# Decayed attention and two gated layers on one core: turns for VectorE and GpSimd in the planner, small products on ScalarE, token sums on VectorE

## The chip, the core and the metric

One core of a Trainium2 chip runs the whole program. The time is device microseconds of one execution. PE is TensorE, PEld its weight load, DVE VectorE, ACT ScalarE, POOL GpSimd and SP SyncE, which issues the DMAs. The tolerance on the result is that of a float32 computation, so every matmul operand is split into a high half that TensorE keeps exactly and a low half for the rest, and each product is made of three matmuls.

## What is computed

Inputs are q, k, v (2 batches, 8 heads, 768 tokens, 64 features), a decay per head, and the weights of two layers (512 to 2048 and back), all in float32 or, for the weights, wider.

```python
# decayed attention, by blocks; lam is one number per head
intra = (q_b @ k_b.T * decay_mask) @ v_b
inter = (q_b * lam_pow) @ kv_state
out_b = intra + inter
kv_state = lam_block * kv_state + (k_b * rev_pow).T @ v_b
# first layer, on 1536 tokens x 512
h = x @ w_in;  g = h * clip(h + 3, 0, 6) / 6;  x = g @ w_out
# second layer
h = maximum(x @ w_in, 0);  y = h * h @ w_out
```

## The kernel before

**Attention** goes through 12 chunks of 128 tokens, two batches in turn. For a chunk TensorE makes the scores (L353), the product of scaled queries with the old state (L385), the product of decayed keys and values for the new state (L403), and scores times values (L437). VectorE masks the scores (L364), adds the new state to the decayed old one (L423), and takes the low half of the chunk's output (L453) after ScalarE has taken a plain copy and the high half (L448, L450). The output bank is one of two, and it is free again only after the low half: so L385 of chunk c + 2 waits for L453 of chunk c. GpSimd scales the queries (`qs`, L327), decays the keys (`kd`, L338, from the second to last chunks of each batch nothing is kept) and decays the old state (`kvs`, L416).

**The layers** take 1536 tokens as three blocks of 512 and w_in and w_out as 64 tiles of 128 x 512 (32 a layer and half a matrix each). A tile comes as 8-byte numbers and is decoded: two reads of the raw words on ScalarE (`da` L513, `dt` L517), a clamp, a shift and a join on VectorE (L522, L528, L532), the high half on ScalarE (L535), an addition and the low half on VectorE (L536, L539). A hidden unit (L666) is 12 matmuls of 512 columns; its gate follows on ScalarE (`gs`, L641) and VectorE (L644), then the halves of the result (L649 ScalarE, L651 VectorE). Four such tiles later the output products (L752) run and are added up in SBUF (L776). From the second group of four on, blocks 0 and 1 are multiplied two by two with sums of weights and of tokens (L697, seven quarter products instead of eight): the weight sums are `Tsum` (L560), `Th`, `Tl` (L573), and the token sums are `s` (L593) with their halves `Ssum` and, for the last, `xh`, `xl` (L609 on GpSimd for the first layer, L611 on VectorE for the second, L613 ScalarE).

**What sets the order.** The kernel is not written in the order of its instructions. `Plan.op` records each with an engine, a cost of `COST` (time the engine is held, time until the result is there), the operations it needs and the buffers it takes and gives. TensorE's order is fixed by hand; `dues` gives every other operation the latest time by which TensorE's order wants it. `run` then walks through time: of all engines the one that can start earliest gets its ready operation with the earliest start, and among those the earliest due. The list that comes out is the order in each engine's queue. At run time each engine works its queue in order and waits on semaphores only for data and buffers. SP's queue holds the loads, a chunk as four DMAs.

Of the kernel before, what the change touches and what calls it, by code (L numbers as in the profile page):

```python
# [9 lines left out]
F32 = mybir.dt.float32  # L10
# [4 lines left out]
AF = mybir.ActivationFunctionType  # L15
ALU = mybir.AluOpType
PSUM = bass.MemoryType.PSUM

P = 128
# [5 lines left out]
    "psc": 1.10, "inter": 1.02, "pst": 0.61, "av": 0.88, "unit": 2.72, "high": 1.81, "low": 0.91, "part": 1.36,  # L25
# [19 lines left out]
class Op:  # L45
    def __init__(self, engine, cost, do, needs, take, give, due, then):
        self.engine, self.do, self.needs, self.take, self.give = engine, do, list(needs), take, give
        cost = COST[cost] if isinstance(cost, str) else cost
        self.busy, self.lasts = cost if isinstance(cost, tuple) else (cost, cost + DRAIN)
        self.due, self.then, self.start, self.end, self.number = due, then, None, None, 0  # L50


class Plan:
# [37 lines left out]
    def run(self):  # L91
# [13 lines left out]
        order, left = [], len(self.ops)  # L105
        while left:
            best = None
            for e in clock:
                if e == "PE":
                    some = [pe[0]] if pe and not waiting[pe[0].number] else []  # L110
                else:
                    some = ready[e]
                first, pick = None, None
                for o in some:
                    t = max(clock[e], o.ready)
                    ok = True
                    for h in o.take:
                        if h.slot is None:
                            if not h.room.free:
                                ok = False  # L120
                                break
                            t = max(t, h.room.free[0][1])
                    if not ok:
                        continue
                    key = (round(t, 3), o.due, o.number)
                    if first is None or key < first:
                        first, pick = key, o
                if pick is not None and (best is None or first[0] < best[0]):
                    best = (first[0], e, pick)
            if best is None:  # L130
                stuck = [(o.engine, o.what) for o in ([pe[0]] if pe else [])]
                raise RuntimeError(f"the plan is stuck: {left} left, {stuck}")
            t, e, o = best
            o.start, o.end = t, t + o.lasts
            clock[e] = t + o.busy
            for h in o.take:
                h.slot = h.room.free.popleft()[0] if h.slot is None else h.slot
# [27 lines left out]
def decay_attention_moe_moe(  # L165
# [134 lines left out]
    def attention():  # L300
# [22 lines left out]
        def prepare(c):  # L323
            if c > 1:

                def do():
                    nc.gpsimd.tensor_tensor(  # L327
                        qs_t[:, qs_hold[c].slot].rearrange("p a i -> p (a i)"), part(c, "q"),
                        lpow_t[0].rearrange("p a i -> p (a i)"), op=ALU.mult,
                    )  # L330

                qs_hold[c] = Hold(qs_room)
                chunk_hold[c].left += 1
                qs_op[c] = op("POOL", "p512", do, [loaded[c, "q"], *scans], take=[qs_hold[c]], give=[chunk_hold[c]])
            if c < NC - 2:

                def do():
                    nc.gpsimd.tensor_tensor(  # L338
                        kd_t[:, kd_hold[c].slot], part(c, "k").rearrange("p (h d) -> p h d", d=D),
                        decay.rearrange("p a t i -> p (a t) i")[:, :, P - 1 : P].to_broadcast([P, H, D]), op=ALU.mult,  # L340
                    )

                kd_hold[c] = Hold(kd_room)
                kd_op[c] = op("POOL", "p512b", do, [loaded[c, "k"], *decays], take=[kd_hold[c]])

# [46 lines left out]
        def new_state(c):  # L392
# [18 lines left out]
            else:  # L411
                s = Hold(ts_room)

                def scale():
                    kvs_t[c] = tile_of([P, KD, HALF], F32, "Ts", f"kvs{c}")[:, :, :D]
                    nc.gpsimd.tensor_tensor(  # L416
                        kvs_t[c], kv_old, lpow_t[0][:, :, P - 1 : P].to_broadcast([P, NP, D]), op=ALU.mult
                    )
# [79 lines left out]
    def decode(n, key, uses, summed, gate):  # L498
# [21 lines left out]
        clamp = op(  # L520
            "DVE", "v512s",
            lambda: nc.vector.tensor_scalar(  # L522
# [4 lines left out]
        shift = op(  # L527
            "DVE", "v512s", lambda: nc.vector.tensor_scalar(u(), u(), 3, None, op0=ALU.logical_shift_left), [clamp]  # L528
        )
        join = op(  # L530
            "DVE", "v512",
            lambda: nc.vector.scalar_tensor_tensor(u(), r(1), -(2**31), u(), op0=ALU.bitwise_and, op1=ALU.bitwise_or),  # L532
            [shift], give=[raw],
        )
        hi = op("ACT", "s512", lambda: nc.scalar.copy(tile_w(0), u().bitcast(F32)), [join], give=[a])  # L535
        add = op("DVE", "v512", lambda: nc.vector.tensor_tensor(up(), u(), up(), op=ALU.add), [join, low], give=[a])  # L536
        lo = op(
            "DVE", "v512",
            lambda: nc.vector.tensor_tensor(tile_w(1), up().bitcast(F32), tile_w(0).bitcast(F32), op=ALU.subtract),  # L539
# [40 lines left out]
    def token_sums(layer, old):  # L580
# [54 lines left out]
    def gate(layer, j, f, ps, done, bank):  # L635
# [10 lines left out]
        else:  # L646
# [3 lines left out]
        lo = op(  # L650
            "DVE", "v512", lambda: nc.vector.tensor_tensor(gt(1), s(), gt(0).bitcast(F32), op=ALU.subtract), [hi], give=[st]  # L651
        )
# [86 lines left out]
    def project(layer, j, g, e):  # L739
# [42 lines left out]
        if layer == 0:  # L782
# [4 lines left out]
            lo = op(  # L787
                "DVE", "v512",
                lambda: nc.vector.scalar_tensor_tensor(  # L789
# [143 lines left out]
```

## Time and profile before

| what | value |
|---|---|
| median of 3 runs | 581.58 us (580.63 to 581.73) |
| profiled execution | 582.72 us, its span 580.9 us |
| TensorE busy | 557.8 us, 96% |
| VectorE busy | 416.0 us, 72% |
| ScalarE busy | 322.5 us, 56% |
| GpSimd busy | 138.3 us, 24% |
| chain that ended last | TensorE 57%, VectorE 28%, ScalarE 7%, GpSimd 2% |

The span runs from the first instruction to the last; the profiled execution's own time has 1.8 us more around it. A busy share is an average over stages with different limits, and a TensorE that is busy is not one at its peak: its matmuls overlap, so a product of 12 matmuls is best read from start to start. The rows that matter are those that say which instruction ended an idle time, stage by stage.

### The profile page before, as it was taken

What the parts mean: (1) busy time and instruction counts of PE and PEld (TensorE: products, weight loads), DVE (VectorE), ACT (ScalarE), POOL (GpSimd) and SP (SyncE); (2) the same over time, 40 slices, a digit from 0 to 9 for tenths busy, and PEclk for the clock granted to TensorE, in tenths of its full rate; (3) what the DMA queues carried; (4) which work ended last, traced back from release to release, by engine and by line L of the source; (5) the groups of instructions that cost most, each with busy time, mean ns of one, the idle gap of its engine ahead of it and who ended that gap; (6) DMA issues with size and microseconds to landing.
All of it is one profiled execution on the core that took longest, in us unless ns stands there. A gap on an engine that the chain in (4) does not pass through costs nothing.

```text
span 580.9 us, 7789 instructions
## 1 busy us (share of the span) xinstructions
PE 557.8 (96%) x2950; PEld 457.3 (79%) x2950; DVE 416.0 (72%) x635; ACT 322.5 (56%) x545; POOL 138.3 (24%) x108
## 2 busy tenths in 40 slices
PE   8969699999999999999999998999999999999997
PEld 5857487888878888788887887888877888888885
DVE  7897999817995599838999886317894589546322
ACT  2524486638751585337763796548862695358220
POOL 4878504301132104201015004201212112210000
PEclk9999799999999999999999999999999999999999
DMA  8990233301231024202231042102231042100112
GB/s 319 408 361 3 73 109 104 113 1 65 81 108 37 0 74 144 73 0 73 73 109 36 21 160 73 37 2 72 73 108 37 0 146 73 37 0 1 63 65 90
DMA packets 18037, 49.79 MB, mean 86 GB/s; under 512 B 2128, under 2 KB 2128, under 8 KB 18000
## 3 DMA queue, kind: packets, MB, share of 16 engines
q1 hardware_dynamic: 17856, 49.04, 24.1%
q8 instruction: 23, 0.38, 0.3%
q10 hardware_dynamic: 144, 0.26, 0.1%
q14 instruction: 14, 0.11, 0.1%
HBM read 46.14 MB, written 3.15 MB: 85 GB/s over the span
## 4 chain that ended last, share of the span: by engine, by line
PE 57%; DVE 28%; ACT 7%; issue 4%; POOL 2%; DVEq 0%; POOLq 0%; ACTq 0%
PE b L752 31%; PE b L697 16%; PE b L666 7%; DVE da L532 4%; DVE dt L536 4%; DVE gs L644 3%; DVE da L528 3%; DVE acc L776 2%; DVE da L522 2%; POOL Tsum L560 1%; DVE wo L539 1%; PE b L353 1%; ACT gs L648 1%; DVE xl L789 1%; DVE A L364 1%
## 5 line engine op out<-in xcount | busy, mean ns | idle before, releaser
L776 DVE TENSOR_TENSOR acc<-acc,b 128x512 f32<-128x512 f32 x72 | 48.6, 681 | 51.9 <-PE b L752 51.9
L666 PE MATMUL b<-xh,wi 128*128 128x512 f32 x240 | 78.6, 398 | 5.4 <-DVE gs L644 5.4
L752 PE MATMUL b<-gC,wo 128*128 128x512 f32 x228 | 70.2, 390 | 1.2 <-DVE gs L644 1.2
L752 PE MATMUL b<-wo,gC 128*128 128x512 f32 x228 | 68.9, 390 | 1.5 <-ACT gC L649 1.5
L666 PEld LDWEIGHTS b<-xh,wi 128*128 128x128 f32 x240 | 46.2, 193 | 15.7 <-DVE gs L644 5.8
L560 POOL TENSOR_TENSOR Tsum<-dt,dt 128x256 f32<-128x256 f32 x12 | 12.7, 1061 | 185.6 <-DVE dt L536 131.2
L573 POOL TENSOR_TENSOR Tl<-Tsum,Th 128x1024 fp32r<-128x1024 f32 x12 | 29.6, 2465 | 111.8 <-ACT Th L568 111.8
L532 DVE SCALAR_TENSOR_TENSOR da<-raw,da 128x512 int32<-128x512 int32 x64 | 50.9, 806 | 1.2
L752 PEld LDWEIGHTS b<-wo,gC 128*128 128x128 f32 x228 | 42.6, 188 | 10.9 <-ACT gC L649 1.9
L752 PEld LDWEIGHTS b<-gC,wo 128*128 128x128 f32 x228 | 42.7, 188 | 10.6 <-DVE gs L644 1.7
L536 DVE CUSTOM_DVE_ANT_0 dt<-da,dt 128x1024 uint16<-128x1024 uint16 x64 | 49.7, 784 | 1.7 <-ACT gs L648 0.2
L647 ACT ACTIVATE gs<-b 128x512 f32<-128x512 f32 x48 | 28.2, 591 | 37.6 <-PE b L666 15.0
L513 ACT ACTIVATE da<-raw 128x512 f32<-128x512 f32 x64 | 42.0, 669 | 11.6 <-issue 6.3
L641 ACT ACTIVATE gs<-b,three 128x512 f32<-128x512 f32 x48 | 32.6, 686 | 27.6 <-PE b L697 16.3
L666 PE MATMUL b<-xl,wi 128*128 128x512 f32 x120 | 47.7, 397 | 0.0
L644 DVE SCALAR_TENSOR_TENSOR gs<-gs,b 128x512 f32<-128x512 f32 x48 | 32.5, 681 | 17.5 <-ACT gs L641 17.3
L517 ACT ACTIVATE dt<-raw 128x512 int32<-128x512 uint32 x64 | 42.6, 667 | 2.1 <-DVE wikd L539 1.1
L651 DVE TENSOR_TENSOR gC<-gs,gC 128x512 fp32r<-128x512 f32 x38 | 29.4, 779 | 18.4 <-ACT gC L649 18.4
L528 DVE TENSOR_SCALAR da<-da 128x512 int32<-128x512 int32 x64 | 40.0, 625 | 1.7
L752 PE MATMUL b<-g,wo 128*128 128x512 f32 x120 | 39.0, 390 | 0.0
L752 PE MATMUL b<-wo,g 128*128 128x512 f32 x120 | 37.6, 389 | 0.0
L752 PE MATMUL b<-gA,wo 128*128 128x512 f32 x108 | 36.3, 390 | 1.1 <-DVE gs L644 1.1
(131 smaller groups left out, 1240.9 us busy)
## 6 DMA issues: line engine op xcount, KB each, us to landing
raw<-in_w_in SPq DMA_DIRECT2D x32, 512.0 KB, 3.3
raw<-in_w_out SPq DMA_DIRECT2D x32, 512.0 KB, 3.3
out<-acc SPq DMA_DIRECT2D x12, 256.0 KB, 2.0
inC<-in_kT SPq DMA_DIRECT2D x6, 256.0 KB, 5.2
inC<-in_k SPq DMA_DIRECT2D x6, 256.0 KB, 5.3
inC<-in_v SPq DMA_DIRECT2D x6, 256.0 KB, 5.4
inS<-in_kT SPq DMA_DIRECT2D x6, 256.0 KB, 5.8
inS<-in_qT SPq DMA_DIRECT2D x6, 256.0 KB, 5.9
```

Of the source, the lines that this page charges most:

```text
L513: "ACT", "s512r", lambda: nc.scalar.activation(abs_t[a.slot], r(1).bitcast(F32), AF.Abs, scale=2.0**16),
L517: "ACT", "s512r", lambda: nc.scalar.activation(up(), r(0).bitcast(U32), AF.Copy, scale=2.0**-29),
L528: "DVE", "v512s", lambda: nc.vector.tensor_scalar(u(), u(), 3, None, op0=ALU.logical_shift_left), [clamp]
L532: lambda: nc.vector.scalar_tensor_tensor(u(), r(1), -(2**31), u(), op0=ALU.bitwise_and, op1=ALU.bitwise_or),
L536: add = op("DVE", "v512", lambda: nc.vector.tensor_tensor(up(), u(), up(), op=ALU.add), [join, low], give=[a])
L573: "POOL", "p1024", lambda: nc.gpsimd.tensor_tensor(at["l"], at["f"], at["h"].bitcast(F32), op=ALU.subtract),
L641: a = op("ACT", "s512b", lambda: nc.scalar.activation(s(), ps(), AF.Relu, bias=three), [done], take=[st])
L644: lambda: nc.vector.scalar_tensor_tensor(s(), s(), 6.0, ps(), op0=ALU.min, op1=ALU.mult), [a], give=bank,
L666: nc.tensor.matmul(ps(), u, x[:, a, :], start=a == 0 and i == 0, stop=a == KD - 1 and i == 2)
L697: nc.tensor.matmul(t, p0, p1, start=start and a == 0 and n == 0, stop=a == KH - 1 and n == 2, skip_group_check=True,)
L752: nc.tensor.matmul(ps(), u, y, start=f == fs[0] and i == 0, stop=f == fs[-1] and i == 2)
L776: "DVE", "v512", lambda: nc.vector.tensor_tensor(t(), t(), ps(), op=ALU.add), [low, old[e]], give=[bank],
```

## The change

Four things change. (1) The planner gets a clock named `port`: an operation on GpSimd, or one on VectorE whose cost name begins with `d`, can start only when the last of these has left it. GpSimd's candidates are dropped where a ready VectorE operation of that kind has an earlier due time and could start before GpSimd's would end. The `d` names go to VectorE's instructions that read and write SBUF alone: the decode steps, the low halves of gates and of the layer's output. (2) The decayed keys become eight ScalarE instructions of 64 columns a chunk, each with a scale read per partition, and the decayed states four. (3) The token sums `s` go from GpSimd to VectorE (four in each layer), and the first layer's low halves too. (4) Costs are renamed or added. Nothing else in the text differs; SP's order is the same.

```diff
+    "d512": (0.60, 0.69), "d512s": (0.36, 0.44), "d256": (0.335, 0.42), "d1024": (1.13, 1.21), "dsums": (1.35, 1.44),
+    "s64x4": (0.50, 0.60), "s64x8": (1.00, 1.10),
...
+        self.port = engine == "POOL" or isinstance(cost_name, str) and cost_name.startswith("d")
...
+        order, left, port = [], len(self.ops), 0.0
+        def earliest(o):
+            t = max(clock[o.engine], o.ready, port if o.port else 0.0)
+            for h in o.take:
+                if h.slot is None:
+                    if not h.room.free:
+                        return None
+                    t = max(t, h.room.free[0][1])
+            return round(t, 3)
...
+                picks = [(t, o.due, o.number, o) for o in some for t in [earliest(o)] if t is not None]
+                if e == "POOL" and picks:
+                    rivals = [(t, o.due) for o in ready["DVE"] if o.port for t in [earliest(o)] if t is not None]
+                    picks = [x for x in picks if not any(d < x[1] and t < x[0] + x[3].busy for t, d in rivals)]
...
+            port = t + o.busy if o.port else port
...
-                    nc.gpsimd.tensor_tensor(
-                        kd_t[:, kd_hold[c].slot], part(c, "k").rearrange("p (h d) -> p h d", d=D),
-                        decay.rearrange("p a t i -> p (a t) i")[:, :, P - 1 : P].to_broadcast([P, H, D]), op=ALU.mult,
-                    )
+                    for h in range(H):
+                        nc.scalar.activation(
+                            kd_t[:, kd_hold[c].slot, h, :], part(c, "k")[:, h * D : (h + 1) * D], AF.Copy,
+                            scale=decay[:, h // 2, h % 2, P - 1 : P],
+                        )
...
-                kvs_op[c] = op("POOL", "p256", scale, [kv_op[c - 2], *scans], take=[s])
+                    for a in range(NP):
+                        nc.scalar.activation(kvs_t[c][:, a, :], kv_old[:, a, :], AF.Copy, scale=lpow_t[0][:, a, P - 1 : P])
+                kvs_op[c] = op("ACT", "s64x4", scale, [kv_op[c - 2], *scans], take=[s])
...
-                nc.gpsimd.tensor_tensor(stage[n], a(), b(), op=sign)
-            return op("POOL", "p1024", do, needs, take=take, give=give)
+                nc.vector.tensor_tensor(stage[n], a(), b(), op=sign)
+            return op("DVE", "d1024", do, needs, take=take, give=give)
...
-                    nc.gpsimd.tensor_tensor(l, stage[n], h.bitcast(F32), op=ALU.subtract)
+                    nc.vector.tensor_tensor(l, stage[n], h.bitcast(F32), op=ALU.subtract)
...
-            lo = op(*(("POOL", "p1024") if layer == 0 else ("DVE", "v1024")), low, [hi], give=[give])
+            lo = op("DVE", "d1024", low, [hi], give=[give])
```

The new text is three lines longer, so a line of the new kernel has a number higher by 3 (by 4 or 5 inside attention). Three places of the order follow.

ScalarE in the middle of attention, before (the decode of the first three w_in tiles, and copy and high half of chunks 3 to 5):

```order
L448 COPY xf_99<-b_66 128x4x128
L450 CAST xh_93<-b_66 128x4x128
L535 CAST wi_112<-da_104 128x512
L513 ACTIVATE da_105<-raw_102 128x512
L517 ACTIVATE dt_107<-raw_102 128x512
L448 COPY xf_100<-b_65 128x4x128
L450 CAST xh_94<-b_65 128x4x128
L513 ACTIVATE da_104<-raw_103 128x512
L517 ACTIVATE dt_108<-raw_103 128x512
```

and now, chunks 3 to 5 as well:

```order
L342 ACTIVATE kd<-inC_84,decay 128x64 x8
L451 COPY xf_99<-b_66 128x4x128
L453 CAST xh_93<-b_66 128x4x128
L421 ACTIVATE kvs_419<-states,lpow 128x64 x4
L538 CAST wi_112<-da_104 128x512
L516 ACTIVATE da_105<-raw_102 128x512
L520 ACTIVATE dt_107<-raw_102 128x512
L451 COPY xf_100<-b_65 128x4x128
L453 CAST xh_94<-b_65 128x4x128
L342 ACTIVATE kd<-inC_85,decay 128x64 x8
```

Each chunk's copy and high half now stand behind the decayed keys and states of later chunks.

VectorE some 20 us after attention, where the first layer's first four tiles of gates end (`gs` the gates, `gA`, `gC` their low halves, `wo` a w_out tile), before:

```order
L644 SCALAR_TENSOR_TENSOR gs_109<-gs_109,b_67 128x512
L539 TENSOR_TENSOR wo_117<-dt_106,wo_117 128x512
L539 TENSOR_TENSOR wo_118<-dt_107,wo_118 128x512
L651 TENSOR_TENSOR gA_135<-gs_109,gA_135 128x512
L651 TENSOR_TENSOR gC_134<-gs_110,gC_134 128x512
L644 SCALAR_TENSOR_TENSOR gs_111<-gs_111,b_68 128x512
L522 TENSOR_SCALAR da_104<-da_104 128x512
L522 TENSOR_SCALAR da_105<-da_105 128x512
L528 TENSOR_SCALAR da_104<-da_104 128x512
L651 TENSOR_TENSOR gA_136<-gs_111,gA_136 128x512
```

and now:

```order
L647 SCALAR_TENSOR_TENSOR gs_109<-gs_109,b_67 128x512
L542 TENSOR_TENSOR wo_118<-dt_107,wo_118 128x512
L596 TENSOR_TENSOR s_962<-s_797,xf_99 128x1024
L654 TENSOR_TENSOR gA_135<-gs_109,gA_135 128x512
L612 TENSOR_TENSOR Ssum_826<-s_797,Ssum_826 128x1024
L596 TENSOR_TENSOR s_981<-xf_99,s_962 128x1024
L647 SCALAR_TENSOR_TENSOR gs_109<-gs_109,b_66 128x512
L596 TENSOR_TENSOR s_999<-xf_99,xf_100 128x1024
L654 TENSOR_TENSOR gC_134<-gs_110,gC_134 128x512
L654 TENSOR_TENSOR gA_136<-gs_109,gA_136 128x512
```

Three sums and one low half of the token sums stand between the gates, and the gate in bank 66 goes ahead of that in bank 68.

VectorE some 60 us later, at the end of the second group, where the gates of the third block (`gs` from banks 63 and 64) meet the decode of the next tiles, before:

```order
L536 ISA dt_106<-da_104,dt_106 128x1024
L539 TENSOR_TENSOR wikd<-dt_108,wikd 128x512
L536 ISA dt_107<-da_105,dt_107 128x1024
L776 TENSOR_TENSOR acc_961<-acc_961,b_65 128x512
L539 TENSOR_TENSOR wo_117<-dt_106,wo_117 128x512
L522 TENSOR_SCALAR da_104<-da_104 128x512
L528 TENSOR_SCALAR da_104<-da_104 128x512
L532 SCALAR_TENSOR_TENSOR da_104<-raw_103,da_104 128x512
L536 ISA dt_108<-da_104,dt_108 128x1024
L539 TENSOR_TENSOR wo_118<-dt_107,wo_118 128x512
L539 TENSOR_TENSOR wi_112<-dt_108,wi_112 128x512
L644 SCALAR_TENSOR_TENSOR gs_111<-gs_111,b_63 128x512
```

and now:

```order
L539 ISA dt_106<-da_104,dt_106 128x1024
L647 SCALAR_TENSOR_TENSOR gs_109<-gs_109,b_63 128x512
L539 ISA dt_107<-da_105,dt_107 128x1024
L542 TENSOR_TENSOR wikd<-dt_108,wikd 128x512
L654 TENSOR_TENSOR g_122<-gs_109,g_122 128x512
L542 TENSOR_TENSOR wo_117<-dt_106,wo_117 128x512
L647 SCALAR_TENSOR_TENSOR gs_111<-gs_111,b_64 128x512
L525 TENSOR_SCALAR da_104<-da_104 128x512
```

The two gates have moved ahead of most of that decode.

## Rows read from the trace of the kernel before

**Rows 1.** Busy time by stretch (us): instructions in brackets, then clock, DMA
```profile
0.00:53.20 53.20, 46.54 (x719) 37.56 (x719) 44.66 (x73) 17.93 (x30) 37.35 (x38) 1.00 0.79 298
53.20:117.64 64.44, 57.66 (x243) 46.86 (x242) 59.34 (x81) 41.10 (x69) 25.76 (x16) 0.95 0.27 90
117.64:577.20 459.56, 453.56 (x1992) 372.87 (x1991) 311.33 (x481) 263.47 (x446) 75.23 (x55) 1.00 0.18 61
```
**Rows 2.** Waits (total us, times, longest); TensorE's timeline (start, us, line, idle before)
```profile
PE b L385 <- DVE xl L453: 5.1, 4, 1.5
...
45.51 1.09 PE L385 MATMUL b<-qs,states 64*64 64x128 f32 x16 [0.68 <-DVE xl L453]
...
49.11 1.09 PE L385 MATMUL b<-qs,states 64*64 64x128 f32 x16
...
53.20 0.50 PE L666 MATMUL b<-xh,wi 128*128 128x512 f32 x1
```
**Rows 3.** Timelines of VectorE and of GpSimd after attention
```profile
56.06 2.52 DVE L528 TENSOR_SCALAR da<-da 128x512 int32<-128x512 int32 x1
...
66.29 0.68 DVE L644 SCALAR_TENSOR_TENSOR gs<-gs,b 128x512 f32<-128x512 f32 x1
66.89 0.68 DVE L532 SCALAR_TENSOR_TENSOR da<-raw,da 128x512 int32<-128x512 int32 x1
...
55.68 2.62 POOL L593 TENSOR_TENSOR s<-xf,s 128x1024 f32<-128x1024 f32 x1
```
**Rows 4.** TensorE's waits after attention, one stretch's clock, a piece of the chain
```profile
67.02 0.79 PE L666 MATMUL b<-xh,wi 128*128 128x512 f32 x1 [5.36 <-DVE gs L644]
...
92.63 0.50 PE L752 MATMUL b<-gdecay,wo 128*128 128x512 f32 x1 [1.42 <-DVE gdecay L651]
...
67.00:72.00 5.00, 4.98 (x12) 3.91 (x13) 4.83 (x9) 3.60 (x6) 0.00 (x0) 0.50 0.31 107
...
117.64 1.36 PE b L697 x6
```
**Rows 5.** ScalarE by form (busy us, mean ns of one); its timeline in attention
```profile
L641 ACT ACTIVATE gs<-b,three 128x512 f32<-128x512 f32 x48 | 32.6, 686 | 27.6 <-PE b L697 16.3 <-DVE b L710 10.2 <-PE b L666 1.2
...
L647 ACT ACTIVATE gs<-b 128x512 f32<-128x512 f32 x48 | 28.2, 591 | 37.6 <-PE b L666 15.0 <-PE b L697 12.5 <-DVE b L710 10.2
...
L649 ACT CAST g<-gs 128x512 fp32r<-128x512 f32 x20 | 12.3, 621 | 4.9 <-DVE gs L644 4.7
...
L568 ACT CAST Th<-Tsum 128x1024 fp32r<-128x1024 f32 x12 | 12.5, 1043 | 1.7 <-POOL Tsum L560 1.7
...
23.72 0.63 ACT L535 CAST wi<-da 128x512 fp32r<-128x512 f32 x1 [1.53 <-DVE da L532]
24.25 0.69 ACT L513 ACTIVATE da<-raw 128x512 f32<-128x512 f32 x1
...
25.39 0.58 ACT L448 COPY xf<-b 128x512 f32<-128x512 f32 x1
25.86 0.61 ACT L450 CAST xh<-b 128x512 fp32r<-128x512 f32 x1
```
**Rows 6.** GpSimd's second decayed keys (timeline); 1024-column sums on GpSimd and VectorE (by form)
```profile
9.20 1.06 POOL L338 TENSOR_TENSOR kd<-inC,decay 128x512 f32<-128x512 f32 x1 [2.19 <-DMA inC<-in_k]
...
L609 POOL TENSOR_TENSOR Ssum<-s,Ssum 128x1024 fp32r<-128x1024 f32 x3 | 7.7, 2583 | 0.0
...
L611 DVE SCALAR_TENSOR_TENSOR xl<-s,xh 128x1024 fp32r<-128x1024 f32 x1 | 1.2, 1225 | 0.3 <-ACT xh L613 0.3
```
**Rows 7.** Later: TensorE's waits, and VectorE ahead of the first one
```profile
173.18 0.72 PE L752 MATMUL b<-gA,wo 128*128 128x512 f32 x2 [1.14 <-DVE gs L644]
...
237.31 1.20 PE L752 MATMUL b<-gC,wo 128*128 128x512 f32 x4 [1.25 <-DVE gs L644]
...
163.97 2.59 DVE L536 CUSTOM_DVE_ANT_0 dt<-da,dt 128x1024 uint16<-128x1024 uint16 x1
...
172.44 0.68 DVE L644 SCALAR_TENSOR_TENSOR gs<-gs,b 128x512 f32<-128x512 f32 x1
```

More of the change, by code (lines that the diff above doesn't have):

```diff
@@ L25 @@
     "psc": 1.10, "inter": 1.02, "pst": 0.61, "av": 0.88, "unit": 2.72, "high": 1.81, "low": 0.91, "part": 1.36,
[1 row of a table removed]
+    "v512": (0.60, 0.69), "v256": (0.335, 0.42),
+    "d512": (0.60, 0.69), "d512s": (0.36, 0.44), "d256": (0.335, 0.42), "d1024": (1.13, 1.21), "dsums": (1.35, 1.44),
+    "s64x4": (0.50, 0.60), "s64x8": (1.00, 1.10),
     "s512": (0.53, 0.63), "s512r": (0.57, 0.67), "s512b": (0.59, 0.69), "s512p": (0.48, 0.59), "s1024": (0.96, 1.06),
@@ L47, in __init__ @@
         self.engine, self.do, self.needs, self.take, self.give = engine, do, list(needs), take, give
-        cost = COST[cost] if isinstance(cost, str) else cost
+        cost_name, cost = cost, COST[cost] if isinstance(cost, str) else cost
         self.busy, self.lasts = cost if isinstance(cost, tuple) else (cost, cost + DRAIN)
+        self.port = engine == "POOL" or isinstance(cost_name, str) and cost_name.startswith("d")
         self.due, self.then, self.start, self.end, self.number = due, then, None, None, 0
@@ L104, in run @@
                 ready[o.engine].append(o)
-        order, left = [], len(self.ops)
+        order, left, port = [], len(self.ops), 0.0
[7 more added lines that the diff above has]
+            return round(t, 3)
         while left:
@@ L112, in run @@
                     some = ready[e]
[L113 to L129, printed above, removed]
+                picks = [(t, o.due, o.number, o) for o in some for t in [earliest(o)] if t is not None]
+                if e == "POOL" and picks:
+                    rivals = [(t, o.due) for o in ready["DVE"] if o.port for t in [earliest(o)] if t is not None]
+                    picks = [x for x in picks if not any(d < x[1] and t < x[0] + x[3].busy for t, d in rivals)]
+                if picks and (best is None or min(picks)[0] < best[0]):
+                    best = (min(picks)[0], e, min(picks)[3])
             if best is None:
@@ L337, in do @@
                 def do():
-                    nc.gpsimd.tensor_tensor(
-                        kd_t[:, kd_hold[c].slot], part(c, "k").rearrange("p (h d) -> p h d", d=D),
-                        decay.rearrange("p a t i -> p (a t) i")[:, :, P - 1 : P].to_broadcast([P, H, D]), op=ALU.mult,
-                    )
+                    for h in range(H):
[3 more added lines that the diff above has]
+                        )
                 kd_hold[c] = Hold(kd_room)
-                kd_op[c] = op("POOL", "p512b", do, [loaded[c, "k"], *decays], take=[kd_hold[c]])
+                kd_op[c] = op("ACT", "s64x8", do, [loaded[c, "k"], *decays], take=[kd_hold[c]])
         def scores(c):
@@ L520, in decode @@
         clamp = op(
-            "DVE", "v512s",
+            "DVE", "d512s",
             lambda: nc.vector.tensor_scalar(
@@ L527, in decode @@
         shift = op(
-            "DVE", "v512s", lambda: nc.vector.tensor_scalar(u(), u(), 3, None, op0=ALU.logical_shift_left), [clamp]
+            "DVE", "d512s", lambda: nc.vector.tensor_scalar(u(), u(), 3, None, op0=ALU.logical_shift_left), [clamp]
         )
         join = op(
-            "DVE", "v512",
+            "DVE", "d512",
             lambda: nc.vector.scalar_tensor_tensor(u(), r(1), -(2**31), u(), op0=ALU.bitwise_and, op1=ALU.bitwise_or),
@@ L535, in decode @@
         hi = op("ACT", "s512", lambda: nc.scalar.copy(tile_w(0), u().bitcast(F32)), [join], give=[a])
-        add = op("DVE", "v512", lambda: nc.vector.tensor_tensor(up(), u(), up(), op=ALU.add), [join, low], give=[a])
+        add = op("DVE", "d512", lambda: nc.vector.tensor_tensor(up(), u(), up(), op=ALU.add), [join, low], give=[a])
         lo = op(
-            "DVE", "v512",
+            "DVE", "d512",
             lambda: nc.vector.tensor_tensor(tile_w(1), up().bitcast(F32), tile_w(0).bitcast(F32), op=ALU.subtract),
@@ L650, in gate @@
         lo = op(
-            "DVE", "v512", lambda: nc.vector.tensor_tensor(gt(1), s(), gt(0).bitcast(F32), op=ALU.subtract), [hi], give=[st]
+            "DVE", "d512", lambda: nc.vector.tensor_tensor(gt(1), s(), gt(0).bitcast(F32), op=ALU.subtract), [hi], give=[st]
         )
@@ L787, in project @@
             lo = op(
-                "DVE", "v512",
+                "DVE", "d512",
                 lambda: nc.vector.scalar_tensor_tensor(
```

3 lines of the change are left out of this document (removed), and 1 row of the table COST.

## The prediction

> **What bounds the kernel now.** I read the busy times by stretch first. TensorE is at work 453.56 of the 459.56 us between 117.64 and 577.20, so little can be won there; it loses time in the two stretches before that [rows 1]. What ends its idle time there comes next. In the attention stretch the product of the queries with the state (L385) waits four times for VectorE's low half (L453), 5.1 us in all; a chunk with no further wait takes 3.60 us (45.51 to 49.11), and attention gives way to the first product with w_in at 53.20 [rows 2]. VectorE is the late engine because GpSimd stands in its way: L528 takes 2.52 us beside a GpSimd instruction of 2.62 us, and four decode instructions pass like that before the first gate (L644) can start at 66.29, though its neighbours follow each other in 0.60 us [rows 3]. TensorE waits 5.36 us for that gate, runs the next 5 us at a granted clock of 0.50 (its lower level, 1.2 GHz, after that idle time), and waits 1.42 us for a low half at 92.63 [rows 4]. So the bound up to 117.64 is VectorE blocked by GpSimd; later it is TensorE, with single waits of 1.1 to 1.3 us [rows 7].
>
> **GpSimd is relieved.** The ten decayed keys (1.06 us where nothing blocks them), the eight decayed states and twelve 128x1024 sums leave it [rows 6]; it keeps the scaled queries in attention and the weight sums later. Between 53.2 and 67 it then has nothing to run, so the four blocked decode instructions take what they take alone. DMA order on SP's queue does not change. The cost is on the two engines that take the work over.
>
> **ScalarE takes 112 small instructions.** No row has a 128x64 ACTIVATE with a scale read per partition, so I bound one. From 512 to 1024 columns a cast goes from 621 to 1043 ns, 0.824 ns a column, so 448 columns fewer save 0.369 us. An operand read per partition costs 686 - 591 = 95 ns (L641 against L647). A 512-column cast from SBUF lets the next start after 0.53 us (23.72 to 24.25) [rows 5]. Lower end, the operand free: 0.53 - 0.369 = 0.161 us. Upper end, no overlap: 0.621 + 0.095 - 0.369 = 0.347 us. I take the start-to-start distance plus the operand, 0.256 us, since the operand's price was seen on this engine; the planner's table has 0.125. The page "ScalarE: Activation LUTs" of the Trainium skill (What ACT_TABLE_LOAD costs) has 186 ns + 0.833 ns a column, 93 ns per such operand, and 93 ns of overlap: 0.239 us here, with which the sum below would end 1.6 us lower; no row shows it.
>
> With 0.256 us ScalarE sets attention's pace. Its order puts nine decayed keys (72 instructions) and six decayed states (24) between the arrival of the second chunk's keys at 9.20 [rows 6] and the high half of chunk 7, with eight pairs of copies at 2 x 0.47, three pairs of decode steps at 1.14 and one cast at 0.53 [rows 5]: 96 x 0.256 + 7.52 + 3.42 + 0.53 = 36.0 us; I put no idle time between, since 1 MB chunks come in less than the 3.6 us that TensorE takes for one. So chunk 7's high half ends at 45.2, VectorE's low half about 0.8 us later, and L385 of chunk 9 starts at 46.1. Before it started at 45.51, and 7.69 us later came 53.20 [rows 2]; so attention ends at 53.8, **+0.6 us**. VectorE's wait for a slow decayed state delays the masks queued behind it, which are not yet due. At the lower end ScalarE needs 26.9 us, is no bound, and the four waits go: 53.20 - 5.1 = 48.1. At the upper end it needs 44.8 us: 62.5.
>
> **From attention to the first sums.** From 53.20 to 117.64 TensorE runs 20 units of 2.72 us (12 products; six stand as 1.36 us [rows 4]), 54.4 us. The stretch is 64.44 us, so 10.0 us are lost: 5.36, 1.42, the low clock (12 products in 5.0 us instead of 2.7) and small change. With the block gone, one sum and a dozen instructions of 0.6 us or less stand between the last masks and the end of the first gate, about 7 us; its bank is wanted by the fourth unit, 8.2 us after attention, so the 5.36 us and the clock come back. What is late next is VectorE, which gets the token sums: 1.2 us each [rows 6]. The tightest place is the low half gA_136, which the first output product needs. In the new order it stands nine instructions behind the seventh gate: 4 x 1.2 + 6 x 0.60 = 8.4 us. The seventh unit ends at 53.8 + 7 x 2.72 = 72.8, its gate starts 0.7 us later, so the low half is there at 81.9. It is wanted after ten units and two thirds of one, 53.8 + 27.2 + 1.8 = 82.8. On time by 0.9 us, if VectorE is not behind at the seventh gate: I keep 0.5 us of the loss, **-9.5 us**, bounds -10.0 and -7.2 (if the 1.42 us and as much again remain).
>
> **Later.** At 173.18 and 237.31 TensorE waits 1.14 and 1.25 us for the gate of the third block, which before stands behind nine decode instructions that follow the L536 of 163.97 (itself blocked to 2.59 us) and ends at 173.1 [rows 7]. The new order sets this gate right behind that L536, up to 5 us earlier. What it overtakes is wanted only behind the output products that this gate opens. **-2.4 us**. The weight sums on GpSimd still start when their data are there, so blocks in this stretch remain. All that TensorE idles there is 459.56 - 453.56 = 6.0 us [rows 1]; bounds -5 and, as a new order can also put a gate late, +2.4.
>
> **Sum.** The profiled execution took 582.72 us with a span of 580.9; + 0.6 - 9.5 - 2.4 = -11.3 gives 571.4. The median of the runs, 581.58, is 1.1 below that execution: **570.3 us**.
>
> **Rivals.** *ScalarE is cheap* (0.16 us): attention ends at 48.1 and everything moves up by 5.7 us: 564.6. For it: short instructions may overlap more than long ones; against it: the 95 ns.
> *The turns do not happen.* They exist in the planner's arithmetic alone: between VectorE and GpSimd the program has no more waits than the data ask for, so each engine issues when its data are there. If VectorE meets GpSimd at other places than planned, the late waits stay (+2.4) and 1.5 us more of the early loss: 574. For it: L528 was blocked for one whole GpSimd instruction [rows 3]. The page "SBUF — State Buffer" of the Trainium skill (Who interferes with whom) says the same, whoever issues first holds the shared pair for its whole instruction; the trace agrees (2.52 us beside 2.62).
> *ScalarE is dear* (0.347 us, no overlap): attention ends 8.7 us later than forecast, 579.0. For it: ScalarE then works without a break; against it: the overlap of 0.09 us that the rows show.
> *Dear, and TensorE's clock falls*, the one that ends slower: with a pace of 5.9 us a chunk TensorE idles 2.3 us in each. If that brings the lower level, the 3.6 us of work take 7.2, 1.3 us more than the pace, in nine chunks 11.7 us: 590.7. It decides from three such chunks on. For it: the fall after 5.36 us of idle time; against it: waits of up to 1.5 us in attention left the clock at 1.00 [rows 1, 2].
>
> **How the numbers follow.** Forecast 0.45 (567 to 573), turns that do not happen 0.21 (573 to 577), cheap ScalarE 0.18 (563 to 567), dear ScalarE 0.08 (577 to 582, a quarter of it within 0.2%, about what a measurement of this kernel can tell from no change), dear with a low clock or weights come too late through the new order 0.08 (slower). Faster 0.87, within 0.2% 0.04, slower 0.09. The range 564 to 577 leaves out the top 0.16 and a little of the bottom.
>
> **What would show it.** ScalarE's small instructions at 0.25 us start to start and ScalarE busy without gaps from 20 to 45 us; L385 still waiting for the low half, by 1 to 1.5 us a chunk; attention ending near 54; no wait over 1 us and a clock of 1.00 between 54 and 108, where the first quarter-size products should start; the gate waits near 164 and 228 gone. I am wrong if attention ends below 50 or above 58, if TensorE idles between 54 and 75, or if the 460 us after that grow by more than 1 us.

## The result, and the profile after

The change takes 566.07 us (565.54 to 567.05, four runs) against 581.11 us for the kernel before on the same chip: ratio 0.9745, 95% interval 0.9724 to 0.9766, 15.0 us faster. The forecast was 11.3 us faster. The profiled executions differ by 17.2 us (582.72 and 565.54; spans 580.9 and 563.7), since that of before lies above its median and that of after below; the stages below are compared between these two. In the changed kernel every line from the decayed keys on is three to five higher, inside attention too: L385 is L389, L416 is L421, L453 is L456, L644 is L647, L697 is L700, L752 is L755.

The page after, busy time per engine and the chain that ended last, then a piece of that chain, and then busy time by stretch, as in [rows 1]:

```profile
PE 554.6 (98%) x2950; PEld 458.0 (81%) x2950; DVE 398.7 (71%) x647; ACT 348.4 (62%) x657; POOL 89.2 (16%) x78
...
PE 94%; ACT 5%; DVE 0%; issue 0%
...
108.16 1.36 PE b L700 x6
...
0.00:53.47 53.47, 48.09 (x719) 39.15 (x719) 37.91 (x73) 42.55 (x141) 13.66 (x18) 0.97 0.79 296
53.47:108.16 54.69, 54.69 (x243) 45.33 (x242) 52.83 (x82) 40.21 (x66) 9.06 (x5) 1.00 0.26 87
108.16:560.00 451.84, 451.82 (x1992) 373.57 (x1991) 307.31 (x493) 265.63 (x451) 66.53 (x55) 1.00 0.19 64
```

From 53.47 to the last matmul TensorE has no idle time left: 54.69 of 54.69 and 451.82 of 451.84 us. VectorE has all but left the chain (28% before, 0% now), and the only other engine with a share of it is ScalarE, in attention. The middle stretch ends in both kernels at the same piece of the chain, the first six matmuls of the quarter products (117.64 in [rows 4], 108.16 now; TensorE has 243 matmuls in it both times). Against [rows 1] attention grew by 0.27 us, the stretch to the first quarter products went from 64.44 to 54.69 (-9.75), the rest from 459.56 to 451.84 (-7.72), and the 3.70 us behind it stayed: together -17.2.

What TensorE still waits for, by the view of its waits (total us, times, longest); the row of L298 is the start of the program:

```profile
PE b L389 <- DVE xl L456: 3.7, 4, 2.1
PE b L298 <- DVE idle L237: 1.5, 1, 1.5
PE b L357 <- DMA inS<-in_qT: 0.2, 1, 0.2
```

The other two rows lie in attention. The longest wait, on TensorE's timeline, and the clock around it (the stretch's busy PE and count, PEld, DVE, ACT, POOL, then granted clock, DMA share, GB/s):

```profile
34.65 0.51 PE L389 MATMUL b<-qs,states 64*64 64x128 f32 x5 [1.05 <-DVE xl L456]
...
44.21 1.97 PE L389 MATMUL b<-qs,states 64*64 64x128 f32 x16 [2.06 <-DVE xl L456]
...
48.28 1.16 PE L357 MATMUL b<-inC 64*128 64x128 f32 x16
...
53.47 0.50 PE L669 MATMUL b<-xh,wi 128*128 128x512 f32 x1
...
38.00:44.20 6.20, 4.00 (x70) 3.32 (x69) 4.83 (x10) 6.20 (x26) 1.28 (x1) 1.00 0.37 129
44.20:47.40 3.20, 3.19 (x36) 2.87 (x38) 3.10 (x6) 2.06 (x7) 1.08 (x1) 0.50 0.31 122
```

Why that low half is late, on ScalarE (its timeline and two groups by form: busy us, mean ns of one) and on VectorE (timeline):

```profile
22.25 2.03 ACT L342 ACTIVATE kd<-inC,decay 128x64 f32<-128x64 f32 x8
24.16 0.59 ACT L451 COPY xf<-b 128x512 f32<-128x512 f32 x1
...
42.71 0.63 ACT L453 CAST xh<-b 128x512 fp32r<-128x512 f32 x1
...
L342 ACT ACTIVATE kd<-inS,decay 128x64 f32<-128x64 f32 x48 | 12.1, 365 | 0.0
...
L421 ACT ACTIVATE kvs<-states,lpow 128x64 f32<-128x64 f32 x32 | 8.7, 373 | 0.0
...
43.37 0.69 DVE L456 TENSOR_TENSOR xl<-b,xh 128x512 fp32r<-128x512 f32 x1 [0.31 <-ACT xh L453]
```

ScalarE is busy through all 6.20 us before the wait ends. VectorE was idle 0.31 us for its high half, and TensorE then stood 2.06 us for VectorE. So the engine named in TensorE's wait is not the late one; the row of VectorE passes the question on to ScalarE. One decayed-key instruction shows as 365 ns, but eight of them stand 1.91 us apart (22.25 to 24.16), 0.24 us each.

After attention VectorE keeps up. Its timeline around the first gate, around the seventh gate and at the low half `gA` that the prediction called the tightest place, with TensorE's row that wants it:

```profile
57.01 0.42 DVE L525 TENSOR_SCALAR da<-da 128x512 f32<-128x512 f32 x1
57.46 0.43 DVE L531 TENSOR_SCALAR da<-da 128x512 int32<-128x512 int32 x1
57.80 0.68 DVE L647 SCALAR_TENSOR_TENSOR gs<-gs,b 128x512 f32<-128x512 f32 x1
...
74.69 0.69 DVE L647 SCALAR_TENSOR_TENSOR gs<-gs,b 128x512 f32<-128x512 f32 x1
...
82.22 0.70 DVE L654 TENSOR_TENSOR gA<-gs,gA 128x512 fp32r<-128x512 f32 x1
...
83.06 0.62 PE L755 MATMUL b<-gA,wo 128*128 128x512 f32 x2
```

Decode instructions take 0.42 and 0.43 us where one took 2.52 before [rows 3], and the first gate starts at 57.80 instead of 66.29.

### The profile page after: what moved, and what is told of

It is laid out like the page before. It is cut to its first block, busy times and chain, and to the rows that moved or that the text cites. A ratio compares the mean times of both kernels' runs of the same rounds, so it can differ in the third digit from the quotient of the medians.

```text
span 563.7 us, 7855 instructions
## 1 busy us (share of the span) xinstructions
PE 554.6 (98%) x2950; PEld 458.0 (81%) x2950; DVE 398.7 (71%) x647; ACT 348.4 (62%) x657; POOL 89.2 (16%) x78
## 4 chain that ended last, share of the span: by engine, by line
PE 94%; ACT 5%; DVE 0%; issue 0%
PE b L755 46%; PE b L669 23%; PE b L700 20%; ACT kd L342 2%; PE b L357 1%; PE b L440 1%; PE b L389 1%; PE b L298 1%; ACT kvs L421 1%; PE b L407 1%; ACT xh L453 1%; ACT xf L451 0%; ACT da L516 0%; ACT dt L520 0%; DVE xl L456 0%
## 5 line engine op out<-in xcount | busy, mean ns | idle before, releaser
L669 PE MATMUL b<-xh,wi 128*128 128x512 f32 x240 | 76.6, 389 | 0.0
L755 PE MATMUL b<-gC,wo 128*128 128x512 f32 x228 | 70.0, 389 | 0.0
L755 PE MATMUL b<-wo,gC 128*128 128x512 f32 x228 | 68.7, 389 | 0.0
L563 POOL TENSOR_TENSOR Tsum<-dt,dt 128x256 f32<-128x256 f32 x12 | 15.7, 1308 | 276.2 <-DVE dt L539 142.6
L644 ACT ACTIVATE gs<-b,three 128x512 f32<-128x512 f32 x48 | 32.6, 685 | 29.0 <-PE b L700 16.5
L755 PEld LDWEIGHTS b<-gC,wo 128*128 128x128 f32 x228 | 42.8, 188 | 8.9
L755 PEld LDWEIGHTS b<-wo,gC 128*128 128x128 f32 x228 | 42.8, 188 | 8.9
L539 DVE CUSTOM_DVE_ANT_0 dt<-da,dt 128x1024 uint16<-128x1024 uint16 x64 | 43.4, 689 | 1.4 <-ACT gs L651 0.2
L647 DVE SCALAR_TENSOR_TENSOR gs<-gs,b 128x512 f32<-128x512 f32 x48 | 32.7, 687 | 11.2 <-ACT gs L644 11.2
L654 DVE TENSOR_TENSOR gC<-gs,gC 128x512 fp32r<-128x512 f32 x38 | 27.3, 726 | 18.1 <-ACT gC L652 18.1
L755 PE MATMUL b<-g,wo 128*128 128x512 f32 x120 | 38.9, 389 | 0.0
L755 PE MATMUL b<-wo,g 128*128 128x512 f32 x120 | 37.6, 389 | 0.0
L755 PE MATMUL b<-gA,wo 128*128 128x512 f32 x120 | 37.6, 389 | 0.0
L755 PE MATMUL b<-wo,gA 128*128 128x512 f32 x108 | 36.2, 389 | 0.0
```

The lines of the kernel that those rows point to most:

```text
L539: add = op("DVE", "d512", lambda: nc.vector.tensor_tensor(up(), u(), up(), op=ALU.add), [join, low], give=[a])
L644: a = op("ACT", "s512b", lambda: nc.scalar.activation(s(), ps(), AF.Relu, bias=three), [done], take=[st])
L647: lambda: nc.vector.scalar_tensor_tensor(s(), s(), 6.0, ps(), op0=ALU.min, op1=ALU.mult), [a], give=bank,
L669: nc.tensor.matmul(ps(), u, x[:, a, :], start=a == 0 and i == 0, stop=a == KD - 1 and i == 2)
L755: nc.tensor.matmul(ps(), u, y, start=f == fs[0] and i == 0, stop=f == fs[-1] and i == 2)
```

## The experiments

All are timed against the kernel before, with times as medians and 95% intervals of the ratio. Diffs are against the changed kernel. The kernel before, timed beside each group of them, had medians from 581.11 to 582.26 us, so a difference between kernels of two groups is good to about 1 us.

### The two halves of the change, one at a time

The planner alone, with the decayed keys, decayed states and all token sums back on GpSimd:

```diff
-kd_op[c] = op("ACT", "s64x8", do, ...)      # eight ACTIVATEs
+kd_op[c] = op("POOL", "p512b", do, ...)     # one tensor_tensor on GpSimd
-kvs_op[c] = op("ACT", "s64x4", scale, ...)
+kvs_op[c] = op("POOL", "p256", scale, ...)
-return op("DVE", "d1024", do, ...)          # token sums
+return op("POOL", "p1024", do, ...)
-lo = op("DVE", "d1024", low, ...)
+lo = op(*(("POOL", "p1024") if layer == 0 else ("DVE", "d1024")), low, ...)
```

> The planner's turns and the d costs alone; decayed keys and states and all token sums are GpSimd's again. Theory A (the moved work makes the gain in the 64 us after attention, the order makes it later): the four token sums on GpSimd block VectorE again after attention, TensorE waits 3 to 6 us between 58 and 72 and the clock falls behind it; attention ends between 50 and 54; the later 6 us come back. 571 to 577 us. Theory B (the turns in the plan make the gain, wherever the work runs): 569 us or less, with no wait over 1 us after attention.

Measured: 588.60 us, 1.0108 (1.0081 to 1.0136), slower than before, which neither theory had expected. TensorE's timeline has two long waits behind attention, which ends at 54.38; VectorE and GpSimd tell of the first, ScalarE of the second:

```profile
71.23 0.79 PE L669 MATMUL b<-xh,wi 128*128 128x512 f32 x1 [5.67 <-DVE gs L647]
...
107.62 1.22 PE L755 MATMUL b<-g,wo 128*128 128x512 f32 x2 [8.71 <-ACT acc L770]
...
61.94 2.50 DVE L531 TENSOR_SCALAR da<-da 128x512 int32<-128x512 int32 x1
...
61.58 2.57 POOL L596 TENSOR_TENSOR s<-xf,s 128x1024 f32<-128x1024 f32 x1
...
106.44 0.66 ACT L520 ACTIVATE dt<-raw 128x512 int32<-128x512 uint32 x1 [0.77 <-DVE wo L542]
107.00 1.54 ACT L770 COPY acc<-b 128x512 f32<-128x512 f32 x3
```

The blocks after attention are those of before (2.50 beside 2.57 us): in the plan the two engines take turns, in the program they meet. The 8.71 us are new. The first copies of output sums (L770) write the tile that the token sums read (`xf`), so the plan may set them only behind those sums; on the chip the last sum that reads it ended at 66.7, but the copies stood in ScalarE's queue behind decode steps and started at 107.00.

The moves alone, with no turns in the plan:

```diff
-self.port = engine == "POOL" or isinstance(cost_name, str) and cost_name.startswith("d")
+self.port = False
```

> The work moved as in the change, but the planner has no port (VectorE and GpSimd are planned as free of each other, costs as in the change). Theory A: attention ends at 53 to 54 and the early gain of about 9.5 us stays; of the later 6 us a part is lost: 567 to 571 us. Theory B: waits for blocked gates return after attention and later: 574 us or more.

Measured: 574.37 us, 0.9879 (0.9855 to 0.9904). The gain after attention is there: 57.56 to 113.17 is 55.6 us, 0.9 above the change's 54.69. But attention ends 4.1 us later than in the change: the plan put token sums into it, and TensorE waits there four times, 6.6 us in all. So the time falls into theory B's range, but not for theory B's reason: of blocked gates only four waits of 0.3 us come back, all of them later. The early stretch is won by the moves, and the order decides on attention and on small waits later.

The keys and states on ScalarE, but all token sums and their first-layer low halves back on GpSimd (the last two edits of the first diff):

> The change with all token sums (eight sums, four low halves) on GpSimd again; keys and states stay on ScalarE, turns stay. Theory A: the block after attention returns, 4 to 9 us lost between 54 and 108, later up to 2.5 us: 571 to 577 us. Theory B: within 2 us of the change, 565 to 568.

Measured: 591.83 us, 1.0170 (1.0150 to 1.0191), the worst of all and above both theories' ranges, with the same long wait:

```profile
PE b L755 <- ACT acc L770: 7.6, 1, 7.6
PE b L389 <- DVE xl L456: 6.7, 3, 3.4
PE b L669 <- DVE gs L647: 2.1, 2, 1.3
```

So the long wait comes with the token sums on GpSimd. The part of the planner that could do this is the rule that drops GpSimd's candidates. It was taken out of the plan alone and out of the change:

```diff
-if e == "POOL" and picks:
-    rivals = [(t, o.due) for o in ready["DVE"] if o.port ...]
-    picks = [x for x in picks if not any(...)]
```

> The planner-only kernel without the rule that drops GpSimd's candidates when VectorE has something due earlier; the port clock and the d costs stay, all work where it was before. Theory C (that rule plans GpSimd's token sums, and with them ScalarE's first copies of the output sums that wait for them, too late, and the fixed order keeps ScalarE's copies late although GpSimd runs early): the wait of 8.7 us on ScalarE's copy near 100 us is gone, 576 to 581 us. Theory D (the port clock itself makes the plan worse): 584 us or more with the wait still there.

> The change without that rule, port clock and moved work as they are. Theory C: with the sums off GpSimd the rule has little left to delay, within 1.5 us of the change: 565 to 568 us. Theory D says that the rule is what helps later: 569 us or more, gate waits near 164 and 228 back.

Measured: the plan alone without the rule 575.03 us, 0.9886 (0.9862 to 0.9909), 13.6 us better than with it and with no wait for the first copies: the first of them is at row 74 of ScalarE's order instead of 85. Attention ends at 48.90 there, with keys and states on GpSimd. The stretch behind it is not won: up to the first quarter product it takes 65.6 us, with one wait of 4.0 us for a decoded w_out tile and three of about 1 us for gates. Since the token sums are on GpSimd here and the decayed keys and states are done before that stretch, its gain points to the token sums. The change without the rule takes 566.54 us, 0.9742 (0.9716 to 0.9768), the same as the change; its order differs in two places on VectorE, where one instruction changes sides with three decode steps, and in one swapped pair on ScalarE. So the rule costs 13.6 us where GpSimd has its old work, by setting ScalarE's copies late in the plan, and does next to nothing in the change, where GpSimd has few instructions to hold back.

Only the second layer's four sums back on GpSimd:

```diff
-nc.vector.tensor_tensor(stage[n], a(), b(), op=sign)
+(nc.vector if layer == 0 else nc.gpsimd).tensor_tensor(stage[n], a(), b(), op=sign)
-return op("DVE", "d1024", do, ...)
+return op(*(("DVE", "d1024") if layer == 0 else ("POOL", "p1024")), do, ...)
```

> Only the second layer's four token sums on GpSimd again. Theory A says that this move, which I did not cost, brought the 2.5 us that TensorE waited near the change of layers (312 and 351 in the kernel before): 568 to 569 us, with one or two waits of over 1 us between 295 and 340. Theory B (the order brought them): 565.5 to 567, no such wait.

Measured: 569.00 us, 0.9785 (0.9765 to 0.9804), 2.9 us above the change. Two waits come back on TensorE's timeline, here first of the kernel before, then of this one:

```profile
310.81 0.39 PE L752 MATMUL b<-gstates,wo 128*128 128x512 f32 x1
312.22 0.72 PE L752 MATMUL b<-gdecay,wo 128*128 128x512 f32 x2 [1.02 <-DVE acc L776]
...
315.09 0.39 PE L666 MATMUL b<-xh,wi 128*128 128x512 f32 x1
...
350.77 0.50 PE L752 MATMUL b<-wo,gC 128*128 128x512 f32 x1 [1.52 <-ACT gC L649]
```

```profile
300.12 1.20 PE L755 MATMUL b<-gA,wo 128*128 128x512 f32 x4 [0.53 <-DVE acc L779]
...
338.55 0.73 PE L755 MATMUL b<-wo,gC 128*128 128x512 f32 x2 [1.41 <-ACT gC L652]
```

### Who sets attention's pace

Theory: ScalarE, with its small instructions. Rival: VectorE or the loads. Three kernels change ScalarE's work. In the first and the third the cost in the plan goes with it, so that the order changes too; in the second the order stays. First, one instruction of 512 columns a chunk instead of eight of 64, by a constant, which leaves out the decay of the keys:

```diff
-for h in range(H):
-    nc.scalar.activation(kd_t[...][:, h, :], part(c, "k")[:, h * D : (h + 1) * D], AF.Copy, scale=decay[...])
+nc.scalar.activation(kd_t[...], part(c, "k"), AF.Copy, scale=0.5)
-kd_op[c] = op("ACT", "s64x8", do, ...)
+kd_op[c] = op("ACT", "s512", do, ...)
```

> The change with each chunk's decayed keys made by one 512-column ACTIVATE with a constant scale instead of eight of 64 columns with a scale per partition; the decay of the keys is left out (a constant 0.5 stands for it). ScalarE saves 1.92 - 0.53 = 1.4 us a chunk. Theory A (ScalarE sets the pace of attention in the change): attention ends at 48 to 50, the rest as in the change, 560 to 563 us. Theory B (VectorE or the DMAs set it): attention ends at 52.5 or later, 565 to 567 us.

Measured: 560.29 us, 0.9635 (0.9603 to 0.9668); attention ends at 48.38 with one wait, 0.33 us, for a load. Second, the same eight instructions twice over:

```diff
-for h in range(H):
+for h in [*range(H), *range(H)]:
```

> The change with each decayed key made twice over, 16 small instructions a chunk instead of 8 (the same values written again). Theory A: eight more instructions at 0.24 us a chunk, nine chunks before the high half of chunk 7, so attention ends 9 x 1.92 = 17 us later, near 70, and the total is near 583 us (more, if TensorE's clock falls in the longer waits). Theory B: 570 us or less.

Measured: 584.92 us, 1.0055 (1.0033 to 1.0078); attention ends at 73.39, 19.9 us later, for 80 more instructions that at 0.24 us make 19.2. ScalarE is the pace, and the rest of the program simply follows later. TensorE's clock falls at times (by stretch: 0.91 and 0.90), as it does once in the change.

Third, the decayed keys as one instruction of VectorE, `kd` as 128x512, which is a kernel of use:

```diff
-for h in range(H):
-    nc.scalar.activation(kd_t[...][:, h, :], ...)
+nc.vector.tensor_tensor(kd_t[...], part(c, "k")..., decay....to_broadcast([P, H, D]), op=ALU.mult)
-kd_op[c] = op("ACT", "s64x8", do, ...)
+kd_op[c] = op("DVE", "d512", do, ...)
```

> The change with the decayed keys as one 128x512 instruction on VectorE instead of eight on ScalarE; states stay on ScalarE. VectorE gets 10 x 0.6 us in attention, ScalarE loses 10 x 1.92. Theory A: attention ends at 48 to 50.5, 560.5 to 564 us. Theory B (VectorE sets the pace): attention ends later than 53.5, 566 us or more.

Measured: 561.46 us (561.24 to 561.69), 0.9655 (0.9623 to 0.9688), better than both kernels and 4.6 us below the change. Its attention and the 54.40 us behind it by stretch, and the new instruction by form:

```profile
0.00:48.12 48.12, 46.01 (x718) 37.18 (x718) 43.44 (x80) 24.13 (x60) 14.09 (x18) 1.00 0.85 319
48.12:102.52 54.40, 54.38 (x240) 44.70 (x239) 52.52 (x80) 40.13 (x65) 9.05 (x5) 1.00 0.28 97
...
L341 DVE TENSOR_TENSOR kd<-inS,decay 128x512 f32<-128x512 f32 x6 | 5.2, 872 | 0.1
```

ScalarE works 24.13 us in attention instead of 42.55, VectorE 43.44 instead of 37.91, and in attention neither is waited for: what is left there are two waits for loads, 0.24 and 0.16 us. One of 0.70 us for ScalarE (L710) comes later, at 107.93. The decayed states moved as well:

```diff
-kvs_op[c] = op("ACT", "s64x4", scale, ...)
+kvs_op[c] = op("DVE", "d256", scale, ...)     # and kd as above
```

> As the last, and the decayed states on VectorE too, one 128x256 instruction each (8 x 0.34 us). Theory A: within 1 us of the last, since ScalarE is no longer the bound: 560 to 564 us. Theory B: slower than the last by 2 us or more.

Measured: 563.20 us, 0.9684 (0.9644 to 0.9723). That is 1.7 us more than the last, a little over the 1 us of theory A. Attention ends at 48.50, so nothing more is won there, and a wait of 1.35 us at 78.75 and one of 0.44 us at 80.62 come with the new order.

### The planner told the truth

The planner counts eight small instructions as 1.00 us. It was given what they take:

```diff
-"s64x4": (0.50, 0.60), "s64x8": (1.00, 1.10),
+"s64x4": (0.96, 1.06), "s64x8": (1.92, 2.02),
```

> The change with the planner told what the small instructions cost (0.96 and 1.92 us instead of 0.50 and 1.00). Theory A: ScalarE holds attention to the same length whatever the plan believes, 52 to 54.5 for its end, 564.5 to 567.5 us. Rival: the wrong cost makes the plan put the work in a poor order, and attention ends before 51: 563.5 us or less.

Measured: 573.33 us, 0.9857 (0.9831 to 0.9883), worse than with the wrong figure, which neither theory had expected. One wait does it, on TensorE's timeline, with VectorE's and ScalarE's:

```profile
55.50 1.33 PE L389 MATMUL b<-qs,states 64*64 64x128 f32 x10 [10.10 <-DVE states L426]
...
40.47 1.25 DVE L596 TENSOR_TENSOR s<-xf 128x1024 f32<-128x1024 f32 x1
...
52.06 1.22 DVE L612 TENSOR_TENSOR Ssum<-s,Ssum 128x1024 fp32r<-128x1024 f32 x1
...
53.38 1.06 ACT L421 ACTIVATE kvs<-states,lpow 128x64 f32<-128x64 f32 x4 [1.30 <-DVE Ssum L612]
```

With attention planned longer, the plan found room for the first token sums at 40.47. Their stage and the decayed state share a buffer (`Ts`), so the last decayed states had to wait until VectorE's low half at 52.06 freed it, and the states, and TensorE, with them.

## Why the prediction held, step by step

**Attention, +0.6 us: right, +0.27, the closeness by luck.** ScalarE sets the pace, as three kernels show, and the attention's end was forecast at 53.8 and came at 53.47. But the size has two errors that nearly cancel. The step from start to start is 0.24 us and not 0.256, which over the 96 instructions is 1.5 us less, and the second chunk's keys began at 8.7 instead of 9.20, right behind the first chunk's. So the high half of chunk 7 ended at 43.34 instead of 45.2, and L389 of chunk 9 started at 44.21 instead of 46.1, 1.9 us early. Against that, from there to the end it is 9.26 us (44.21 to 53.47) and not the 7.69 of [rows 2], 1.6 us more. Nearly all of it lies in the stretch at half the clock that followed the wait of 2.06 us: from L389 to the next scores (L357) it is 4.07 us (44.21 to 48.28), where the kernel before took 2.51 (45.51 to 48.02). I had put a fall of the clock only into the dear rival. It is not in every execution: of the four that were timed three had a mean granted clock of 0.996 or 0.997, and one, at 567.05 us, had 1.000. The waits for the low half are not even, as I had them, but 0.47, 1.05, 0.15 and 2.06 us. The page "ScalarE: Activation LUTs" of the Trainium skill (What ACT_TABLE_LOAD costs) gives, as an estimate by its formula, 0.239 us; the trace, which had no such row before, now agrees with 0.24. The lower end of that term, an attention of 48.1, is what ScalarE's relief gives (48.12 and 48.38).

**From attention to the first sums, -9.5 us: right, -9.75.** TensorE idles nowhere in this stretch any more (64.44 to 54.69). The low half `gA` started at 82.22 and ended at 82.92, 1.0 us later than I worked out, since the seventh gate came at 74.69 and not at 73.5. It was in time: its group of products begins at 82.61, but with other gates, two tiles named `gA` come last in it, at 83.06 and one step of 0.23 us later, and this one is the second: wanted at 83.29, 0.37 us after its end. So the 0.5 us that I kept were for the most part not needed, but the margin is thinner than the 0.9 us that I read.

**Later, -2.4 us: the way right, the size too small, -7.72.** This is the mis-sized term, and it lies outside my bound of -5. It has three causes. First, the waits of 1.14 and 1.25 us at the third block's gates [rows 7] are gone by the order, as I argued: they are gone in the plan alone too, where no work is moved. (The moves alone, in another order, leave four of 0.3 us in their place.) Two waits that I did not count, of 0.4 and 0.7 us at 426 and 438 in the kernel before, are also the order's: they stand in the moves alone (0.41 and 0.65 us) and in no kernel that was planned with turns. Second, the waits of 1.02 and 1.52 us around the change of layers are gone as well. I had moved the second layer's four sums off GpSimd in the text and given that no price; put back, they cost 2.9 us and bring 0.53 and 1.41 us of these waits back, and the other kernels with these sums on GpSimd have two such waits too (0.56 to 0.82 and 1.39 to 1.83 us), those with the sums on VectorE none for `gC`. Third, I priced a wait at its idle time alone. In the rows shown of before, the matmul of 312.22 follows that of 310.81 after 1.41 us where 0.23 is the step, a loss of 1.18 for 1.02 us of idle time, and the twelve matmuls from 312.22 to 315.09 take 2.87 instead of 2.72. That is 0.3 us more for a wait, and the five others lose as much: by the starts of the same matmuls in the two traces the six cost 1.46, 1.56, 1.33, 1.82, 0.69 and 0.98 us, 7.84 for 6.0 us of idle time. The change itself loses 0.3 us at 112.25 that the kernel before does not. One trace of each kernel is kept, and the two lie 2.1 us further apart than the medians, so a part of these sizes belongs to the two executions.

**The rivals.** The measured 566.07 lies in the band of 563 to 567 that I gave to *ScalarE cheap*, and not in the forecast's own 567 to 573: by the number alone that rival would have won. The stages rule it out, since attention ended at 53.47 and not at 48.1; what was missing came later. *ScalarE cheap* had the mechanism of a real kernel, only not of this one: the keys on VectorE give its attention. *The turns do not happen* is half true. They are not kept at run time: in the change there is still a block, on VectorE's and GpSimd's timelines

```profile
101.40 2.57 POOL L576 TENSOR_TENSOR Tl<-Tsum,Th 128x1024 fp32r<-128x1024 f32 x1 [4.48 <-ACT Th L571]
...
101.62 2.89 DVE L542 TENSOR_TENSOR wi<-dt,wi 128x512 fp32r<-128x512 f32 x1
```

and in the plan alone four in a row from 59.28 on. But the late waits did not stay with it, because VectorE has little left to meet. The two *dear* rivals are out with 0.24 us; of the second, the fall of the clock itself was seen, once for 3.2 us in the change and several times with twice the keys, where the program comes out slower than before (584.92).

**What I did not see.** The gain is not a sum of parts. The planner's half alone costs 6.5 us, the moves alone bring 7.8, both bring 15.0. I had treated the order as an effect of its own; it depends on who holds the token sums.

**Why near-identical orders differ.** Attention ends at 53.47 in the change, at 53.94 with the second layer's sums back and at 55.12 without the rule, in the profiled executions. The difference is there from the start: ScalarE's first instruction, the load of its table, waits for the keys of the first chunk until 5.49, 5.99 and 6.80 us. From there ScalarE works through the same work without a gap, and L389 of chunk 9 starts at 44.21, 44.74 and 45.51, as much later (the last 0.35 of the 55.12 comes behind it). The load on ScalarE's timelines, the change first and the kernel without the rule last, and that L389 on TensorE's timeline of the last, where it is L386:

```profile
5.49 1.28 ACT L342 ACT_TABLE_LOAD   x1 [5.49 <-DMA inC<-in_k]
...
5.99 1.28 ACT L342 ACT_TABLE_LOAD   x1 [5.99 <-DMA inC<-in_k]
...
6.80 1.28 ACT L339 ACT_TABLE_LOAD   x1 [6.80 <-DMA inC<-in_k]
...
45.51 1.14 PE L386 MATMUL b<-qs,states 64*64 64x128 f32 x16 [2.06 <-DVE xl L453]
```

**Open.** Why the first keys land at other times was not found. Keys and states back on GpSimd with the sums on VectorE was not tried; the 48.90 of the plan without the rule speaks for it.

## What to carry to other kernels

When a wait names an engine, look at what that engine waited for itself, and count the instructions of the engine at the end of that line: eight small instructions at 0.24 us were dearer than one large one at 0.7 to 0.9 us on another engine that had room. A planner's rule has to be tried with the work it was made for: the same three lines cost 13.6 us with the old work on GpSimd and next to nothing without it, and a truer cost made a worse order, so an order is judged by its trace. And every instruction that a change moves needs a term in the sum, in the later stages too. A time that lands near the forecast does not show that its terms were right: here it lay in a rival's band, and only the stages told the two apart.

## What the runs showed of the hardware

A wait of 2.06 us in attention was followed by 3.2 us at a granted clock of 0.50, while waits of up to 1.5 us in the kernel before [rows 1, 2] left the attention at 1.00. The length of one wait does not tell it: with all token sums back on GpSimd, TensorE waited 0.74 us at 92.61 and 1.08 us at 95.12, and the clock fell there too:

```profile
88.00:95.34 7.34, 5.52 (x24) 3.95 (x23) 5.30 (x7) 4.00 (x7) 2.38 (x1) 1.00 0.01 2
95.34:98.75 3.41, 3.41 (x9) 2.63 (x9) 3.33 (x8) 1.65 (x3) 0.00 (x0) 0.50 0.00 0
```

Each of six single waits of TensorE cost about 0.3 us more from start to start than its idle time. A 128x64 ACTIVATE with a scale read per partition shows as 349 to 373 ns and lets the next one start after 0.24 us.

The table load of ScalarE moved from 1.17 us in the kernel before to 5.49 us: in the change it waits for the keys' data, like the decayed key behind it (rows above), and its 1.28 us stand at the head of the work that sets attention's pace. A load ahead of a key does not always wait for it: with keys made by a constant, a decayed key is the first ACTIVATE as well and waits for its data, but the load is done long before:

```profile
6.69 0.63 ACT L341 ACTIVATE kd<-inC 128x512 f32<-128x512 f32 x1 [4.24 <-DMA inC<-in_k]
```

There the load stands at 1.17 us, as in the kernel before. That key reads no decay; whether this makes the difference is not shown. An earlier load in the change was not tried.
